# Weight loads on SyncE's queue and threshold rows on GpSimd's in a fused attention and feed-forward kernel

## The chip, the cores and the metric

The kernel runs on one core of a Trainium2 chip. The metric is device time in microseconds (us) of one execution, the median of several. Engines are named as in the profile: PE (TensorE matmul), PEld (its weight loads), DVE (VectorE), ACT (ScalarE), POOL (GpSimd), SP (SyncE, which here only issues DMAs). A DMA is issued by an engine's instruction; the transfer itself runs on 16 DMA engines that all queues share.

## The reference, cut to what matters

```python
# q, k, v: (8, 8, 576, 64) float32; tau = 0.02
scale = 1.0 / np.sqrt(q.shape[-1])
scores = scale * np.matmul(q, k.transpose(0, 1, 3, 2))
thresh = np.max(scores, axis=-1, keepdims=True) - tau
scores = np.where(scores >= thresh, scores, -1000000000.0)
scores = scores - np.max(scores, axis=-1, keepdims=True)
attn = np.exp(scores)
attn = attn / (np.sum(attn, axis=-1, keepdims=True) + 1e-09)
attn_out = np.matmul(attn, v)
# (B, H, S, D) -> x: (4608, 512)
h = x @ w_in                                  # w_in:  (512, 2048)
g = h * (1.0 / (1.0 + np.exp(-1.702 * h)))
out = g @ w_out                               # w_out: (2048, 512)
```

`w_in` and `w_out` reach the kernel as 64-bit floats and are made 32-bit on the chip.

## The kernel before

**Attention** goes by pairs of heads: 8 batches of 4 pairs, 32 pairs n = 0 to 31. For each pair SP loads q and k (`load_qk`, four DMAs of 72 KB each, in pieces of 128 bytes; only k of pair 0 is issued by ACT) and v (`load_v`, four of 144 KB). DVE transposes q and k (`prep`, L502). PE makes the transposed scores in nine tiles of 64 keys (`scores`, L518), ACT copies them out of PSUM (`keep`, L535), DVE takes maxima over keys (`in_groups`, L541; `over_tiles`, `over_halves`). The row of thresholds must then stand in every partition: `turn_rows` (L585) transposes it, `row_out` (L631, two DMAs) writes it to DRAM, `row_in` (L640, two DMAs of 144 KB) reads it back into all partitions, tile `mb`. Pair 2 does this on DVE alone (`spread_max`). DVE subtracts it (`sub`, L646, five instructions per pair), ACT masks and exponentiates (`mask` L652, `exps` L656). PE multiplies with v (`values`, L667, tile `pv`). Sums over keys come from PE for pairs 0 to 4 (`sums_by_pe`, tile `den`; DVE then `one_row`, `spread_sums`), later from DVE, and then their reciprocals go out and in through DRAM too (`sums_out` L734, `sums_in` L741). `place_x` (L769) writes the normalised result as a part of x, tile `xT`.

**Weights** come in 32 pieces of 128 x 512 values, 512 KB each, 16 of `w_in` first. `load_w` (L451) issues one from GpSimd into a staging place: eight halves of stages in the tile `w_out` and four places (`w64`) in `arena`. Six steps make a piece 32-bit: `cv_ex` (L459), `cv_frac` (L477), `cv_join` (L484) and `cv_end` (L491) on DVE, `cv_power` and `cv_power2` (L466, L470) on ACT. A place is free for the next piece after `cv_end`. The first six loads wait for `hold`, a one-column copy on GpSimd that reads k of pair 3 after its transpose.

**Feed-forward** goes by blocks of 256 tokens. The first two blocks (`first_blocks`) need pairs 0 to 3 placed and the weights: 128 matmuls of `mm1_0` (L824), 16 activations (`tanh` on ACT, `gelu_0` on DVE, L830), 64 matmuls of `mm2` (L806). After them ACT and GpSimd form sums of `w_out` (`t_minus` L931; `t_plus` L935, a DMA that adds, issued by GpSimd). The following blocks (`feed_forward`, L784 and L796; `second`, L975, with DVE reads at L997) use a scheme with seven products in place of eight and GpSimd sums (L941 to L954); the last four blocks use it in both layers. Block b begins when the pairs of its batch are placed.

**Order.** Nothing of this order is written out by hand. Each step is a `task` with an engine, an assumed cost, a rank, the tasks that it follows, and buffers that it takes and gives back. `run_in_order` plays the whole kernel with these costs, and on each engine issues the ready task of the lowest rank. So the instruction order on every engine is fixed when the program is built, and on the chip each engine runs its list in order, waiting by semaphores. The rank of an attention task is the pair's number plus a bias by step (tables `EARLY`, `SECOND`, `LATER` for pairs 0 to 3, 4 to 7, and later ones), that of a weight task comes from `W_RANK` plus a bias of table `CV`. Transfers are played on two assumed movers, "DMS" for SP's queue and "DMW" for GpSimd's, which share by `SHARE` when both are busy.

From pair 4 on q and k of pair n are loaded after the row of pair n - 2 has been issued (`behind`). From pair 7 on the scores of pair n are interleaved with the values of pair n - 2 (`JOINT`).

Of the kernel before, what the change touches and what calls it, by code (L numbers as in the profile page):

```python
# [30 lines left out]
def kernel(  # L31
# [83 lines left out]
    gap = const.tile([P, 1], FP32, name="gap")  # L115
    stop = const.tile([P, 1], FP32, name="stop")
    minus = const.tile([P, 2, KT], FP32, name="minus")
# [11 lines left out]
    for x in ("raw0", "raw1", "qkT0", "qkT1", "mb"):  # L129
# [5 lines left out]
    EARLY = {  # L135
        "exps": -4.07,
        "in_groups": 22.01,
        "keep": -79.06,
        "load_qk": 12.29,
        "load_v": 22.73,  # L140
        "mask": -2.64,
        "one_row": 11.94,
        "over_halves": -68.94,
        "over_tiles": -10.94,
        "place_x": -9.91,
        "prep": 31.46,
        "row_in": 266.46,
        "row_out": -20.89,
        "scores_run": -78.01,
        "spread_max": 21.18,  # L150
        "spread_sums": -40.19,
        "sub": 20.98,
        "sums_by_pe": 115.71,
        "turn_rows": 8.92,
        "values": 5.45,
        "w_sum": -2.55,
    }
    SECOND = {
        "exps": -5.9,
        "in_groups": 272.61,  # L160
        "keep": 24.39,
        "load_qk": 24.22,
        "load_v": 275.36,
        "mask": 21.81,
        "one_row": 3.96,
        "over_halves": 26.26,
        "over_tiles": -69.17,
        "place_x": 24.28,
        "prep": 26.2,
        "row_in": 3.22,  # L170
        "row_out": 27.26,
        "scores_run": 11.9,
        "spread_sums": -33.61,
        "sub": 26.97,
        "sums_by_pe": -17.24,
        "sums_in": -40.32,
        "sums_out": -33.4,
        "turn_rows": 86.46,
        "turn_sums": 113.15,
        "values": -68.38,  # L180
    }
    LATER = {
        "exps": -16.87,
        "in_groups": 287.56,
        "keep": -81.02,
        "load_qk": -69.87,
        "load_v": -9.77,
        "mask": 15.33,
        "over_halves": 8.05,
        "over_tiles": -2.37,  # L190
        "place_x": -12.35,
        "prep": -40.12,
        "row_in": 27.6,
        "row_out": -2.41,
        "scores_run": 27.98,
        "sub": 29.43,
        "sums_in": -21.09,
        "sums_out": -40.82,
        "turn_rows": -18.77,
        "turn_sums": -16.08,  # L200
        "values": -68.99,
        "x_sum": -2.89,
    }
    CV = {
        "cv_end": 29.51,
        "cv_ex": 20.82,
        "cv_frac": 114.8,
        "cv_join": -10.06,
        "cv_power": 12.8,
        "cv_power2": 5.12,  # L210
        "load_w": -4.52,
    }
# [18 lines left out]

    SHARE = (0.22, 0.6)

# [205 lines left out]
    def load_w(i):  # L439
        dst, src, c, j = pieces[i]  # L440
        dram = src[ts(c, P), ts(j, WC)]
        if not wide:
            nc.gpsimd.dma_start(out=dst[:, c, ts(j, WC)], in_=dram)
            return
        at = staged(i)
        if at in W64:
            t = arena[:, ts(W64.index(at), 2 * WC)]
        else:
            t = w_out[:, ts(HALVES.index(at), 2), :].rearrange("p a b -> p (a b)")
        t = t.bitcast(U32)  # L450
        nc.gpsimd.dma_start(out=t, in_=dram.bitcast(U32), max_dma_last_dim=1024)  # L451
        t = t.rearrange("p (c w) -> p c w", w=2)
        cv[i] = t[:, :, 1], t[:, :, 0], dst[:, c, ts(j, WC)]
# [41 lines left out]

    held_k = {}
    mats, sT, stats, mbs, rows, pss = {}, {}, {}, {}, {}, {}

    def prep(n, which):

        dst = home(n, f"qkT{which}")
        nc.vector.transpose(out=dst, in_=raws.pop((n, which)))  # L502
        mats[n, which] = dst
        if which:
            held_k[n] = dst

    def hold(n):

        nc.gpsimd.tensor_copy(out=stop, in_=held_k[n][:, 0:1])

# [115 lines left out]


    def row_out(n):
        rows[n] = dram.tile([2, S], FP32, name="row", tag="row", bufs=2)
        for c in range(2):  # L630
            nc.sync.dma_start(  # L631
                out=rows[n][c : c + 1].rearrange("o (g i) -> (o g) i", i=32),
                in_=flat[1][ds(c * KT, QB)],
            )

    def row_in(n):
        mb = home(n, "mb")
        row = rows.pop(n)
        for c in range(2):
            nc.sync.dma_start(out=mb[ts(c, KT)], in_=row[c : c + 1].to_broadcast([KT, S]))  # L640
        mbs[n] = mb
# [89 lines left out]
    def sums_out(n):  # L731
        rcs[n] = dram.tile([2, 2, SH], FP32, name="row_s", tag="row_s", bufs=2)
        for c in range(2):
            nc.sync.dma_start(  # L734
                out=rcs[n][c].rearrange("h (g i) -> (h g) i", i=32), in_=flat_s[1][ds(c * KT, QB)]
            )

    def sums_in(n):
        rc, row = seat("rc"), rcs.pop(n)
        for h in range(2):  # L740
            nc.sync.dma_start(  # L741
                out=rc[ts(h, D)].rearrange("p (c s) -> p c s", c=2),
# [309 lines left out]
    SUMS_BY_DMA = range(5, NP)  # L1052
    LEAD = 6
    WHOLE = 6

# [3 lines left out]

    W_RANK = (21.04, 13.12, 21.54, 8.44, 155.39, -7.77)  # L1060
    W_TIME = 1.9
    ready_w, w_loads = [], []
    for i in range(len(pieces)):
# [7 lines left out]
        place = (staged(i),)  # L1071
        a = task("POOL", 0.6, rank, load_w, i, after=w_loads[-1:], take=place)
        w_loads.append(a)
        a = transfer("DMW", W_TIME, a)

# [177 lines left out]
    lvs = []  # L1253
    exped, loaded, summed = {}, {}, {}

# [21 lines left out]
    for n in range(NP):  # L1277
# [145 lines left out]
        if n not in SUMS_BY_PE:  # L1423
# [5 lines left out]
            if n in SUMS_BY_DMA:  # L1429
                a = task("DVE", 1.46, r, turn_sums, n, after=[a], take=("row_s",))  # L1430
                a = transfer("DMS", 0.3, task("SP", 0.65, r, sums_out, n, after=[a]))
                a = task("SP", 1.2, r, sums_in, n, after=[a], take=("rc",))
                summed[n] = transfer("DMS", 0.7, a, 1, give=("row_s",))
            else:
# [42 lines left out]
```

## Time and profile before

| What | us |
|---|---|
| Runs shown: median (lowest to highest, 3 runs) | 1313.77 (1311.2 to 1315.54) |
| Profiled execution, its own time | 1316.25 |
| Profiled execution, span from first to last instruction | 1314.4 |
| PE busy in the span | 1261.8 |
| DVE busy | 1007.4 |
| ACT busy | 667.0 |
| POOL busy | 242.7 |
| Granted PE clock, mean over the span | 0.988 |

DMA traffic by queue, in packets, MB and share of the time of 16 DMA engines:

```profile
q1 hardware_dynamic: 180476, 64.30, 20.8%
q0 software_dynamic: 8800, 20.97, 6.1%
```

q1 is the queue of DMAs that SP issues, q0 that of GpSimd's; a third one (q10) carries ACT's one load. Issuing a DMA is not counted as busy time. A matmul that is listed as 128x256 f32 counts twice in the trace, since it runs in two passes. Line numbers in the profile are those of the kernel before.

### The profile page before, as it was taken

The numbers are of one execution on the slowest core, as the hardware profiler recorded it, in microseconds if no ns is written. First come the engines' busy times: TensorE is split into PE (matmuls) and PEld (weight loads), VectorE is DVE, ScalarE is ACT, GpSimd is POOL, SyncE is SP. The second block draws the span as 40 slices with busy tenths as digits, with TensorE's granted clock in tenths as the row PEclk, the third lists the DMA queues.
The fourth block names the chain that finished last, engine by engine and source line by source line (L and its number), as shares of the span: only waits on it lengthen the run. The fifth ranks groups of instructions, "written<-read, shape, count | busy, mean of one in ns | idle before, by whom it ended". The sixth has DMA issues, their size and how long they took to land.

```text
span 1314.4 us, 22775 instructions
## 1 busy us (share of the span) xinstructions
PE 1261.8 (96%) x9128; PEld 980.3 (75%) x9128; DVE 1007.4 (77%) x1601; ACT 667.0 (51%) x862; POOL 242.7 (18%) x269
## 2 busy tenths in 40 slices
PE   5777999999999999999999999999999999999998
PEld 2635764466787777777778887777777778888887
DVE  7899898999987888788787877777887864652642
ACT  4897666876745545555554554454655540210210
POOL 1102010012030211213021302021121217120120
PEclk8888999999999999999999999999999999999999
DMA  6724356453322222112222222222122110000000
GB/s 125 230 65 151 79 175 109 98 119 73 89 64 71 55 55 71 46 54 55 57 43 71 55 71 56 71 50 63 44 61 54 31 51 9 9 1 30 3 0 32
DMA packets 191749, 87.01 MB, mean 66 GB/s; under 512 B 159772, under 2 KB 170780, under 8 KB 191644
## 3 DMA queue, kind: packets, MB, share of 16 engines
q1 hardware_dynamic: 180476, 64.30, 20.8%
q0 software_dynamic: 8800, 20.97, 6.1%
q8 instruction: 71, 1.16, 0.4%
q10 hardware_dynamic: 2368, 0.30, 0.2%
q14 instruction: 34, 0.28, 0.1%
HBM read 71.63 MB, written 9.70 MB: 62 GB/s over the span
## 4 chain that ended last, share of the span: by engine, by line
PE 72%; DVE 15%; DMA 6%; ACT 3%; issue 2%; SPq 2%; DVEq 0%; ACTq 0%
PE ops L975 25%; PE hps L784 21%; PE pv L667 8%; PE ps L518 7%; PE ps L889 4%; DVE part L541 4%; PE ps L975 4%; DVE arena L646 3%; PE ops L889 3%; DMA row<-flat 2%; DMA arena<-row 2%; ACT arena L656 1%; DVE arena L502 1%; DMA arena<-in_k_dram 1%; SPq L398 1%
## 5 line engine op out<-in xcount | busy, mean ns | idle before, releaser
L541 DVE TRANSPOSE_TENSOR_REDUCE part<-arena 128x36 f32<-128x1152 f32 (+1 forms) x295 | 357.6, 1237 | 41.7 <-ACT arena L535 32.3
L784 PE MATMUL hps<-xT,w_in 128*128 128x256 f32 x1536 | 337.2, 380 | 1.3 <-DVE arena L796 1.2
L784 PEld LDWEIGHTS hps<-xT,w_in 128*128 128x128 f32 x1536 | 290.6, 190 | 46.9 <-issue 5.7
L652 ACT ACTIVATE arena<-arena 128x1152 f32<-128x1152 f32 (+1 forms) x160 | 169.6, 1060 | 133.1 <-DVE arena L646 132.8
L535 ACT COPY arena<-ps 128x576 f32<-128x576 f32 x288 | 170.8, 647 | 120.8 <-PE ps L518 120.8
L646 DVE TENSOR_TENSOR arena<-arena 128x1152 f32<-128x1152 f32 (+1 forms) x158 | 200.8, 1316 | 21.1 <-DMA arena<-row 20.9
L975 PE MATMUL ops<-w_out,arena 128*128 128x256 f32 x896 | 204.6, 383 | 3.0 <-DVE osb L997 1.9
L656 ACT ACTIVATE arena<-arena,shift,scl 128x1152 f32<-128x1152 f32 (+1 forms) x160 | 200.6, 1254 | 4.0
L518 PE MATMUL ps<-arena 64*64 64x288 f32 x2304 | 175.0, 420 | 23.9 <-DVE arena L502 10.9
L975 PEld LDWEIGHTS ops<-w_out,arena 128*128 128x128 f32 x896 | 170.2, 191 | 31.5 <-DVE arena L796 3.1
L941 POOL TENSOR_TENSOR arena<-arena 128x256 f32<-128x256 f32 x56 | 49.0, 874 | 646.8 <-DVE arena L796 545.1
L667 PE MATMUL pv<-arena 64*64 64x288 f32 x2176 | 159.9, 407 | 0.0
L793 ACT ACTIVATE th<-hps 128x512 f32<-128x512 f32 x112 | 66.2, 591 | 175.2 <-PE hps L784 157.7
L518 PEld LDWEIGHTS ps<-arena 64*64 64x64 f32 x2304 | 87.4, 138 | 86.8 <-ACT arena L535 21.2
L975 PE MATMUL ops<-arena 128*128 128x256 f32 x672 | 150.6, 380 | 0.0
L975 PEld LDWEIGHTS ops<-arena 128*128 128x128 f32 x672 | 127.3, 190 | 19.3 <-issue 2.2
L667 PEld LDWEIGHTS pv<-arena 64*64 64x64 f32 x2176 | 81.6, 133 | 53.9 <-issue 9.6
L997 DVE SCALAR_TENSOR_TENSOR osb<-ops,osb 128x256 f32<-128x256 f32 x98 | 39.4, 414 | 98.4 <-PE ops L975 92.3
L796 DVE SCALAR_TENSOR_TENSOR arena<-th,hps 128x512 f32<-128x512 f32 x96 | 64.4, 670 | 39.4 <-ACT th L793 39.3
L824 PE MATMUL hps<-xT,w_in 128*128 128x256 f32 x256 | 59.1, 390 | 7.4 <-DVE w_in L491 3.7
L824 PEld LDWEIGHTS hps<-xT,w_in 128*128 128x128 f32 x256 | 49.2, 195 | 17.5 <-DVE arena L830 4.9
L909 ACT ACTIVATE th<-arena 128x512 f32<-128x512 f32 x32 | 20.3, 636 | 72.5 <-DVE arena L905 72.5
(118 smaller groups left out, 1085.2 us busy)
## 6 DMA issues: line engine op xcount, KB each, us to landing
arena<-in_v_dram SPq DMA_DIRECT2D x128, 144.0 KB
arena<-in_q_dram SPq DMA_DIRECT2D x128, 72.0 KB
out_dram<-osb SPq DMA_DIRECT2D x36, 256.0 KB
arena<-in_k_dram SPq DMA_DIRECT2D x124, 72.0 KB
arena<-row SPq DMA_DIRECT2D x62, 144.0 KB
arena<-row_s SPq DMA_DIRECT2D x54, 144.0 KB
w_out<-in_moe_w_in_dram POOLq DMA_DIRECT2D x12, 512.0 KB, 7.4
arena<-in_moe_w_out_dram POOLq DMA_DIRECT2D x12, 512.0 KB, 7.5
```

Source lines behind the costliest of these rows:

```text
L518: nc.tensor.matmul(ps[ts(c, KT), h, 0:SH], lhsT=mats[n, 1][ts(h, D), ts(j, KT)], rhs=mats[n, 0][ts(h, D), ts(c, SH)], start=True, stop=True,)
L535: nc.scalar.copy(out=sT[n, t][:, u], in_=pss.pop((n, j))[:, :, 0:SH])
L541: nc.vector.tensor_reduce(out=stats[n, op][:, t * 2 * QB : min(2 * t + 2, NK) * QB], in_=sT[n, t].rearrange("p u h (g d) -> p (u h g) d", ...
L646: engine.tensor_tensor(out=s, in0=s, in1=mbs[n].unsqueeze(1).to_broadcast(list(s.shape)), op=ALU.subtract)
L652: nc.scalar.activation(out=s, in_=s, func=AF.Prelu, alpha=STEEP)
L656: nc.scalar.activation(out=s, in_=s, func=AF.Exp, scale=scl, bias=shift)
L667: nc.tensor.matmul(o[c][ts(h, D), 0:SH], lhsT=left(j, h)[ts(c, KT)], rhs=sT[n, t][ts(c, KT), u, h, :], start=(j == 0), stop=(j == NK - 1),)
L784: nc.tensor.matmul(hidden[j][:, ts(f, BLK)], lhsT=w_in[:, c, ds((f * HF + j) * P, P)], rhs=xTs[blk][:, c, :], start=(c == 0), stop=(c == N ...
L793: nc.scalar.activation(out=ths[j], in_=hidden[j], func=AF.Tanh, scale=GELU_SCALE / 2)
L824: nc.tensor.matmul(hidden[j][:, ts(i, BLK)], lhsT=w_in[:, c, ts(j, P)], rhs=xTs[i][:, c, :], start=(c == 0), stop=(c == NDC - 1),)
L889: nc.tensor.matmul(places[j, x], lhsT=left[:, c, ts(j, P)], rhs=right[:, c, :], start=(c == 0), stop=(c == 1),)
L975: nc.tensor.matmul(banks[blk][k][:, ts(o, HM)], lhsT=left[:, j, :], rhs=right[:, j, :], start=(j == 0), stop=(j == HF - 1),)
```

## The change

- `load_w` issues the weights from SP, in the queue of q, k and v. Its task goes to SP, its transfer to mover "DMS" (kind 2); `SHARE` gets a third entry.
- `hold`, the tile `stop` and the waits for them are gone: the first weights may be loaded from the start.
- `row_queue(n)`: for pairs 0 to 7 `row_out`, `row_in`, `sums_out` and `sums_in` are issued by GpSimd, for later pairs by SP as before.
- `behind`: q and k of pair n wait for the transposes of an earlier pair instead of the row of pair n - 2, where that row is issued by GpSimd or n is 2.
- All biases in `EARLY`, `SECOND`, `LATER` and `CV`, the six numbers of `W_RANK`, and `W_TIME` are other numbers, so the whole order is played anew.

```diff
-    SHARE = (0.22, 0.6)
+    SHARE = (0.15, 0.5, 0.6)
...
-        nc.gpsimd.dma_start(out=t, in_=dram.bitcast(U32), max_dma_last_dim=1024)
+        nc.sync.dma_start(out=t, in_=dram.bitcast(U32))
...
-        if which:
-            held_k[n] = dst
-
-    def hold(n):
-
-        nc.gpsimd.tensor_copy(out=stop, in_=held_k[n][:, 0:1])
...
+    def row_queue(n):
+        return nc.gpsimd if n in ROWS_BY_POOL else nc.sync
+
     def row_out(n):
         rows[n] = dram.tile([2, S], FP32, name="row", tag="row", bufs=2)
         for c in range(2):
-            nc.sync.dma_start(
+            row_queue(n).dma_start(
...
-            nc.sync.dma_start(out=mb[ts(c, KT)], in_=row[c : c + 1].to_broadcast([KT, S]))
+            row_queue(n).dma_start(out=mb[ts(c, KT)], in_=row[c : c + 1].to_broadcast([KT, S]))
...
+    ROWS_BY_POOL = range(8)
     WHOLE = 6
...
-    W_RANK = (21.04, 13.12, 21.54, 8.44, 155.39, -7.77)
-    W_TIME = 1.9
+    W_RANK = (-17.54, -19.75, 3.69, 13.93, 26.33, -28.4)
+    W_TIME = 1.6
...
-        a = task("POOL", 0.6, rank, load_w, i, after=w_loads[-1:], take=place)
+        a = task("SP", 0.65, rank, load_w, i, after=w_loads[-1:], take=place)
         w_loads.append(a)
-        a = transfer("DMW", W_TIME, a)
+        a = transfer("DMS", W_TIME, a, 2)
...
+        rq = ("POOL", 1.4, "DMW", 2.2) if n in ROWS_BY_POOL else ("SP", 1.0, "DMS", 1.7)
...
-        behind = [spread[n - 2]] if n >= NPAIR else []
+        behind = [spread[n - 2]] if n >= NPAIR and n - 2 not in ROWS_BY_POOL else preps[n - 1 if n > 3 else n - 2] if n in (2, *range(4, NP)) else []
...
+        preps.append([pq, pk])
         if n == 0:
             tasks[tau_done][5].extend([pq, pk])
-        if n == 3:
-
-
-            h = task("POOL", 0.3, FIRST, hold, n, after=[pk])
-            for a in w_loads[0:6]:
-                tasks[a][5].append(h)
...
-            a = transfer("DMS", 0.3, task("SP", 0.65, r, row_out, n, after=[a]))
-            spread[n] = task("SP", 1.1, r, row_in, n, after=[a], take=own(n, "mb"))
-            m = transfer("DMS", 0.7, spread[n], 1, give=("row",))
+            a = transfer(rq[2], 0.3, task(rq[0], 0.65 * rq[1], r, row_out, n, after=[a]))
+            spread[n] = task(rq[0], 1.1 * rq[1], r, row_in, n, after=[a], take=own(n, "mb"))
+            m = transfer(rq[2], 0.7, spread[n], 1, give=("row",), lag=rq[3])
```

Left out: the tables of biases (all values replaced) and `sums_out`, `sums_in` with their tasks, changed in the same way as `row_out` and `row_in`. Lists of the built programs show what this does to the order. SP's list now begins with four weight pieces, then q of pair 0, q and k of pair 1, six pieces, q and k of pairs 2 and 3, six pieces, and only then v of pairs 0 and 1. DVE's list begins with the conversion of the first four pieces, then the transposes of pair 0. On PE the 128 matmuls of `mm1_0`, broken up by attention of pairs 4 and 6 before, stand in one run.

More of the change, by code (lines that the diff above doesn't have):

```diff
@@ L115 @@
     gap = const.tile([P, 1], FP32, name="gap")
-    stop = const.tile([P, 1], FP32, name="stop")
     minus = const.tile([P, 2, KT], FP32, name="minus")
@@ L135 @@
     EARLY = {
[L136 to L153, printed above, removed]
@@ L154 @@
-        "turn_rows": 8.92,
-        "values": 5.45,
-        "w_sum": -2.55,
+        "exps": 47.12,
+        "in_groups": 31.3,
+        "keep": 32.74,
+        "load_qk": 29.52,
+        "load_v": 88.91,
+        "mask": 47.59,
+        "one_row": -13.82,
+        "over_halves": 23.69,
+        "over_tiles": -19.38,
+        "place_x": 36.77,
+        "prep": -75.13,
+        "row_in": -12.15,
+        "row_out": 37.49,
+        "scores_run": 5.02,
+        "spread_max": -15.22,
+        "spread_sums": 32.66,
@@ L157 @@
+        "sub": -13.77,
+        "sums_by_pe": 11.61,
+        "turn_rows": -17.79,
+        "values": 9.46,
+        "w_sum": 36.74,
     }
     SECOND = {
[L159 to L180, printed above, removed]
+        "exps": 48.41,
+        "in_groups": 90.77,
+        "keep": -52.88,
+        "load_qk": 12.53,
+        "load_v": 67.07,
+        "mask": 27.44,
+        "one_row": 59.42,
+        "over_halves": 22.95,
+        "over_tiles": 6.12,
+        "place_x": 27.27,
@@ L181 @@
+        "prep": 41.33,
+        "row_in": 35.7,
+        "row_out": 20.9,
+        "scores_run": 30.56,
+        "spread_sums": -25.02,
+        "sub": 67.34,
+        "sums_by_pe": -4.59,
+        "sums_in": 9.14,
+        "sums_out": 58.99,
+        "turn_rows": 12.71,
+        "turn_sums": 66.39,
+        "values": 56.01,
     }
     LATER = {
[L183 to L202, printed above, removed]
+        "exps": 20.37,
+        "in_groups": 85.93,
+        "keep": 12.29,
+        "load_qk": 56.34,
+        "load_v": 4.91,
@@ L203 @@
+        "mask": 45.29,
+        "over_halves": 13.04,
+        "over_tiles": 11.11,
+        "place_x": 43.96,
+        "prep": 29.75,
+        "row_in": -12.01,
+        "row_out": 12.27,
+        "scores_run": 19.69,
+        "sub": 73.39,
+        "sums_in": 27.57,
+        "sums_out": 40.94,
+        "turn_rows": 21.08,
+        "turn_sums": 42.06,
+        "values": -14.78,
+        "x_sum": 62.94,
     }
     CV = {
-        "cv_end": 29.51,
-        "cv_ex": 20.82,
-        "cv_frac": 114.8,
@@ L208 @@
[L208 to L211, printed above, removed]
+        "cv_end": 47.56,
+        "cv_ex": 38.81,
+        "cv_frac": 65.22,
+        "cv_join": 80.5,
+        "cv_power": 48.25,
+        "cv_power2": -13.93,
+        "load_w": 28.32,
     }
@@ L493, in cv_end @@
         )
-    held_k = {}
     mats, sT, stats, mbs, rows, pss = {}, {}, {}, {}, {}, {}
@@ L733, in sums_out @@
         for c in range(2):
-            nc.sync.dma_start(
+            row_queue(n).dma_start(
                 out=rcs[n][c].rearrange("h (g i) -> (h g) i", i=32), in_=flat_s[1][ds(c * KT, QB)]
@@ L740, in sums_in @@
         for h in range(2):
-            nc.sync.dma_start(
+            row_queue(n).dma_start(
                 out=rc[ts(h, D)].rearrange("p (c s) -> p c s", c=2),
@@ L1253 @@
     lvs = []
-    exped, loaded, summed = {}, {}, {}
+    exped, loaded, summed, preps = {}, {}, {}, []
     def valued(n, pv):
@@ L1430 @@
                 a = task("DVE", 1.46, r, turn_sums, n, after=[a], take=("row_s",))
-                a = transfer("DMS", 0.3, task("SP", 0.65, r, sums_out, n, after=[a]))
-                a = task("SP", 1.2, r, sums_in, n, after=[a], take=("rc",))
-                summed[n] = transfer("DMS", 0.7, a, 1, give=("row_s",))
+                a = transfer(rq[2], 0.3, task(rq[0], 0.65 * rq[1], r, sums_out, n, after=[a]))
+                a = task(rq[0], 1.2 * rq[1], r, sums_in, n, after=[a], take=("rc",))
+                summed[n] = transfer(rq[2], 0.7, a, 1, give=("row_s",), lag=rq[3])
             else:
```

## The prediction, made before the changed kernel had run

> **What bounds the kernel now.** I read the page first, its busy times and its 40 slices (32.9 us each).
>
> ```profile
> PE 1261.8 (96%) x9128; PEld 980.3 (75%) x9128; DVE 1007.4 (77%) x1601; ACT 667.0 (51%) x862; POOL 242.7 (18%) x269
> ...
> PE   5777999999999999999999999999999999999998
> ...
> DVE  7899898999987888788787877777887864652642
> ```
>
> PE is full from the fifth slice on; before that DVE is. Busy times of whole stretches fix the border:
>
> ```profile
> 0.00:30.39 30.39, 14.49 (x164) 6.83 (x168) 20.97 (x37) 12.62 (x22) 3.52 (x22) 0.90 0.70 127
> 30.39:116.43 86.04, 62.83 (x849) 39.06 (x841) 77.97 (x133) 79.49 (x99) 8.41 (x12) 0.90 0.45 123
> 116.43:340.00 223.57, 214.87 (x1504) 142.50 (x1505) 209.11 (x335) 149.94 (x194) 35.61 (x38) 0.99 0.53 122
> 340.00:1314.40 974.40, 969.65 (x6618) 791.94 (x6616) 699.34 (x1100) 424.99 (x549) 195.18 (x198) 1.00 0.19 47
> ```
>
> (Columns: stretch, length, busy PE, PEld, DVE, ACT, POOL, granted clock, DMA share, GB/s.) Of PE's 52.6 us without work, 39.1 lie before 116.43, 8.7 before 340, 4.7 in the 974 us after. So only the first 340 us can give or lose much. The timeline of PE says what 116.43 is and what it waited for:
>
> ```profile
> 116.43 22.67 PE L824 MATMUL hps<-xT,w_in 128*128 128x256 f32 x96 [3.73 <-DVE w_in L491]
> 140.94 10.98 PE L824 MATMUL hps<-xT,w_in 128*128 128x256 f32 x48 [1.84 <-DVE arena L830]
> ...
> 296.04 7.17 PE L784 MATMUL hps<-xT,w_in 128*128 128x256 f32 x32 [1.25 <-DVE arena L796]
> ...
> 337.49 5.41 PE L975 MATMUL ops<-w_out,arena 128*128 128x256 f32 x16 [1.89 <-DVE osb L997]
> ```
>
> The first feed-forward matmul starts at 116.43, held by DVE (a weight's last conversion step, L491). DVE is late for its own reasons; its waits up to 345 us:
>
> ```profile
> DVE arena L646 <- DMA arena<-row: 13.8, 5, 5.7
> DVE arena L502 <- DMA arena<-in_q_dram: 7.3, 1, 7.3
> ```
>
> 7.3 us pass before the first q lands; the subtractions (L646) wait five times for threshold rows, 5.7 us for pair 1 at 38.7 to 44.5. In the chain that wait is row out and row in, under the first twelve weights:
>
> ```profile
> 30.81 4.55 DMA row<-flat
> 35.38 8.99 DMA arena<-row
> 44.46 5.83 DVE arena L646 x5
> ```
>
> **What the change leaves alone.** The instruction lists of the two kernels hold the same matmuls with the same 64 switches between attention and feed-forward; before the first feed-forward matmul stand the same scores, sums and values, and from some 285 us of PE work on PE's order is identical. DVE too has the same work in front of it: summing the means of the page's fifth part over DVE's list, 109.7 us in both (placement of pair 3 now; before, the last step of weight piece 0). DVE runs such sums faster than their means: work 48.2 to 109.7 took 59.23 to 116.29, 57.1 us for 61.5, factor 0.93. So the new time is the old, plus the shift of that first matmul, plus the shift of PE's waits behind it.
>
> **Part 1: weights first, in SP's queue.** Four pieces stand ahead of q of pair 0, six more ahead of pair 2, six ahead of v. Removed: POOL's copy (hold, 0.18 us at 29.3) and the wait of weights for pair 3; POOL loses 32 issues of 0.75 us, SP gets them (0.65 by its q rows, 2.13 to 3.37 us for four), 21 us on an engine that otherwise waits.
>
> ```profile
> L451 POOL DMA_DIRECT2D w_out<-in_moe_w_in_dram x12: 751/751/782, 29.8 to 118.9; - x12
> ...
> DMA to landing us min/median/max: 3.8/8.4/14.4
> ```
>
> A lone piece takes 3.8 us from issue, and at the 346 GB/s that the windows give for 120 to 132 us each piece behind it 1.5 us more: landings near 4.6, 6.1, 7.6, 9.1. DVE converts them (0.42 + 0.43 + 0.70 + 0.68 each) in the time in which it waited. q of pair 0 flows behind them: 0.295 MB at 150 GB/s (the window at 4 to 16 us) is 2.0 us; its last DMA waits besides for an earlier one (each of SP's loads waits for the load eight before it, by the list), and k of pair 0, on ACT, now stands behind the first conversion's activation. I take 13.5 us for q landed, first scores at 15 (8.8 before).
> The same arithmetic for the rest: k of pair 1 at 19, six weights flow to 28, q and k of pairs 2 and 3 (2.0 us each plus latency, k of 3 issued by 35.6) land by 37.8. DVE's list puts the transposes of pair 3 ahead of the first subtraction, which so starts near 39.5 (30.39 before): 9.1 later, with 30.3 us of work done against 22.9, worth 7.4 x 0.93 = 6.9. Debt +2.2 us. Bounds: -1.3 (loads land 3.5 us sooner, DVE then held by its own work) to +10 (weights at the 227 GB/s that v reaches at 68 to 70 us, 2.3 us a piece: ten pieces, 0.8 us longer each).
>
> **Part 2: rows by GpSimd.** Pairs 0, 1, 3 to 7 send rows out and in (28 DMAs), pairs 5 to 7 also sums (12): 40 x 0.75 = 30 us on POOL, busy 18%. On SP the trip took 6.0 us from 242.5 (row end to landing) with little else moving and 14.0 for pair 1. On POOL the trace shows none. Lower bound 6; upper 14; between: 2 issues 1.5, landing 3.4 behind the issue (tau's load by GpSimd, 4.1 from its issue), 2 issues 1.5, landing 3.0 (the lone weight's 3.8 less its issue): 9.4. I take 9.4, for it is nearest to calm rows of the same engine. DVE's work between row and subtraction is 9.6, 9.2 and 8.8 us by means, 8.9, 8.6 and 8.2 in time, for pairs 0, 1, 3. Pair 0 hides (its subtraction waits for loads); pairs 1 and 3 wait 0.8 and 1.2. With 1.0 for sums that ACT delivers late (from its first mask near 41 to pair 3's last exponential ACT has 68 us of activations and ends at 109, with 3.5 of sums and placement behind it on DVE), waits come to 3.0 where 5.7 were: -2.7.
> What else sits on POOL: sums in of pair 5 stand behind the first T transfer (L935), which waits for two activations of 1.05 us; placement of pair 5 is 10 us of work later. Nothing, unless that cover goes; then some 2 us on DVE.
> GpSimd's issues meet DVE's work: 32 weight issues took 751 to 912 ns while DVE was 90% busy. The Trainium skill ("SBUF — State Buffer", on DVE blocking DMAs) says the opposite could happen: GpSimd writes descriptors through a port that some DVE instructions lock, 620 ns becoming about 3100. The trace disagrees so far. At 3.1 us for each of a trip's four issues the trip would be 9.4 us longer, by estimate from that page, and the time beyond (b) below, whose chance holds it.
>
> First matmul: 116.4 + 2.2 - 2.7 = **115.9**.
>
> **Part 3: new ranks, behind that.** PE now runs its 128 first-layer products in a row (3.45 us for each activation), with 57.9 x 0.93 = 53.9 us of DVE between first and last of 16 activations against 51.8 of PE: +2.1. Values of pair 5 stand 80.5 us of PE behind the start (89.1 before); with 2.1 for switches and 2.1 of waits PE is there at +84.7, and DVE, which must have summed pair 5 (95.6 us by means, x 0.93), at +88.9: 4.2 more. Beyond, q, k and rows come sooner than before; I take 0.6. Waits 6.9, against 1.84, 1.74, 1.48, 0.34, 1.25, 1.89 (8.5): -1.6. Bounds: 0 and 15 (the three later pairs each wait like pair 5).
>
> **Sum.** -0.5 - 1.6 = -2.1 on the profiled execution's own 1316.25 (span 1314.4 and 1.85 around it): 1314.2. The runs' median lies 2.5 below that execution, so **1311.7**. About 0.3%, 3.9 us, is what a measurement here can tell from no change.
>
> **Rivals.**
> (a) The waits vanish: loads at their early bound and rows hidden, -1.3 - 5.7 = -7.0 for the start, and PE's waits behind it 5.5, -3.0: -10, **1304**. For: DVE idles 14.5 us between 116 and 340, 8.1 of them for rows. Against: DVE and PE run level there, so one holds the other.
> (b) Slower by rows: the trip over GpSimd takes the 14.0 us of pair 1 before, for its packets share the engines with weights as before. Pairs 0, 1, 3 wait 5.1, 5.4, 5.8, 17.3 with the sums in place of 3.0: **1326**; a trip of 12 gives 1320. It decides from 10.3 us, where the sum above is used up; each further us costs three. For: the same two streams met at 31 to 44 us. Against: weights now come in bursts with gaps.
> (c) Slower by the single queue: weights at 235 GB/s, debt +10 for +2.2: **1319.5**, more with a wait for v of pair 0, which stands behind sixteen pieces. It decides from 0.2 us longer a piece. For: in order behind each other, and the eighth-load wait. Against: 4096-byte packets took 188 ns on 16 engines, 349 GB/s.
> (d) The change does not do what it says: "not held back" is taken over by the eighth-load wait, and what is gained at the start DVE takes back in the run of activations: no change, **1313.8**.
>
> **Chances.** Forecast 0.38 (own range 1306 to 1317; of it a third below 1309.8), (a) 0.22, (b) 0.14, (c) 0.14, (d) 0.12. Faster by over 0.3%: 0.12 + 0.22 + 0.03 = 0.37; within: 0.26 + 0.08 = 0.34; slower: 0.28 + 0.01 = 0.29. The range reaches to both sides' cases: 1301 to 1323.
>
> **What would show it.** First scores near 15 us; first subtraction 38 to 41; first feed-forward matmul 113 to 119; DVE's waits for rows up to 345 us under 6 in all; PE's waits from there to 340 near 6. Wrong if that matmul starts before 110 or after 122, if GpSimd's issues take much over 0.75 us, or if PE loses more than 8 us after 340.

## The result: slower by 0.8%

| | median us (lowest to highest, runs) | profiled execution, its span |
|---|---|---|
| before | 1312.08 (1311.2 to 1315.54, 5) | 1316.25, 1314.4 |
| changed | 1322.82 (1320.91 to 1326.52, 5) | 1326.52, 1324.7 |

The ratio is 1.0078, with a 95% interval from 1.0056 to 1.0100: a loss of 10.7 us where a gain of 2.1 was forecast. Both profiled executions lie some 4 us above their medians, so the two traces can be compared with each other.

The page of the changed kernel, busy times and slices of 33.1 us:

```profile
PE 1263.5 (95%) x9128; PEld 973.7 (74%) x9128; DVE 1006.5 (76%) x1601; ACT 665.1 (50%) x862; POOL 236.8 (18%) x276
...
PE   3688999899999999999999999999999999999998
...
DVE  7798997888987888877787877777887873652642
```

The work is the same. PE's first three slices are 3, 6, 8 in tenths. Stretches cut at the same events as in the prediction (first subtraction, first feed-forward matmul, 340 us, end):

```profile
0.00:41.55 41.55, 17.84 (x208) 8.47 (x208) 28.38 (x48) 21.74 (x36) 4.92 (x24) 0.92 0.88 209
41.55:122.25 80.70, 61.03 (x800) 32.67 (x800) 71.74 (x128) 71.37 (x87) 4.33 (x8) 0.87 0.46 117
122.25:340.00 217.75, 206.90 (x1472) 135.07 (x1469) 195.79 (x311) 143.85 (x190) 30.23 (x44) 0.98 0.44 102
340.00:1324.70 984.70, 977.75 (x6654) 797.51 (x6652) 710.63 (x1118) 428.18 (x551) 197.27 (x200) 1.00 0.19 47
```

The third number after the length is DVE's busy time. Up to the first subtraction DVE is not busy for 41.55 - 28.38 = 13.2 us (9.4 before); from there to the first feed-forward matmul for 9.0 (8.1 before). Its work up to that matmul is 100.1 us (98.9 before). So 3.75 + 0.9 + 1.2 = 5.8: the matmul starts at 122.25 instead of 116.43. The timeline of PE from there on (start, length, and in brackets the wait ahead of it with what ended it):

```profile
122.25 55.61 PE L819 MATMUL hps<-xT,w_in 128*128 128x256 f32 x256
196.39 1.98 PE L801 MATMUL ops<-w_out,arena 128*128 128x512 f32 x4 [2.39 <-DVE w_out L490]
258.04 2.20 PE L510 MATMUL ps<-arena 64*64 64x288 f32 x16 [6.02 <-ACT arena L527]
313.31 0.72 PE L510 MATMUL ps<-arena 64*64 64x288 f32 x8 [0.57 <-ACT arena L527]
322.30 3.72 PE L779 MATMUL hps<-xT,w_in 128*128 128x256 f32 x16 [1.17 <-DVE arena L791]
326.68 3.29 PE L970 MATMUL ops<-w_out,arena 128*128 128x256 f32 x14 [0.66 <-DVE arena L791]
351.01 7.17 PE L970 MATMUL ops<-arena 128*128 128x256 f32 x32 [1.14 <-DVE osb L992]
370.88 1.25 PE L510 MATMUL ps<-arena 64*64 64x288 f32 x16 [0.99 <-ACT arena L527]
```

These waits sum to 12.9 us where 8.5 were. 5.8 + 4.4 = 10.2 of the 10.3 us between the two spans: two places hold nearly the whole loss, the start and the stretch to some 370 us. (The feed-forward matmuls that start at 367.28 before start at 376.93 now, 9.65 us later.)

DVE's waits up to 122.25 (total, times, longest):

```profile
DVE w_in L458 <- DMA w_out<-in_moe_w_in_dram: 4.8, 1, 4.8
DVE arena L641 <- DMA arena<-row: 3.7, 2, 3.4
DVE arena L500 <- DMA arena<-in_q_dram: 3.2, 2, 2.0
DVE r L693 <- PE den L662: 3.0, 2, 2.5
DVE arena L500 <- DMA arena<-in_k_dram: 2.5, 3, 1.2
DVE w_in L490 <- ACT w_in L469: 1.7, 1, 1.7
```

Before, one wait of 7.3 for q, one of 1.0 for k and one of 5.7 for a row stood here. Now there are eleven smaller ones, and those for loads and weights come to 12.2 us (4.8 + 3.2 + 2.5 + 1.7).

How far one execution can be trusted here is shown by a run below, a_sums_sync, whose program is the same as the changed kernel's up to that matmul. Its timeline has

```profile
120.00 55.52 PE L819 MATMUL hps<-xT,w_in 128*128 128x256 f32 x256
```

which is 2.25 us sooner, with the first subtraction at 40.97. So differences of some 2 us in this start, between two traces, say nothing, and the loss of the start is 3.6 to 5.8 us.

### The profile page after: what moved, and what is told of

It is laid out like the page before. It is cut to its first block, busy times and chain, and to the rows that moved or that the text cites. A ratio compares the mean times of both kernels' runs of the same rounds, so it can differ in the third digit from the quotient of the medians.

```text
span 1324.7 us, 22760 instructions
## 1 busy us (share of the span) xinstructions
PE 1263.5 (95%) x9128; PEld 973.7 (74%) x9128; DVE 1006.5 (76%) x1601; ACT 665.1 (50%) x862; POOL 236.8 (18%) x276
## 4 chain that ended last, share of the span: by engine, by line
PE 72%; DVE 13%; ACT 7%; DMA 5%; issue 2%; SPq 1%; POOL 0%; DVEq 0%; POOLq 0%
PE ops L970 23%; PE hps L779 20%; PE pv L662 8%; PE ps L510 8%; PE ps L884 4%; DVE part L533 4%; PE ps L970 4%; DVE arena L641 4%; PE ops L884 3%; ACT arena L651 3%; ACT arena L647 2%; ACT arena L527 1%; DMA arena<-row 1%; DMA arena<-row_s 1%; DMA arena<-in_k_dram 1%
## 5 line engine op out<-in xcount | busy, mean ns | idle before, releaser
L779 PE MATMUL hps<-xT,w_in 128*128 128x256 f32 x1536 | 337.0, 380 | 1.2 <-DVE arena L791 1.2
L779 PEld LDWEIGHTS hps<-xT,w_in 128*128 128x128 f32 x1536 | 290.8, 190 | 46.3 <-issue 5.3
L801 PE MATMUL ops<-w_out,arena 128*128 128x512 f32 x128 | 57.1, 599 | 2.4 <-DVE w_out L490 2.4
L949 POOL TENSOR_TENSOR arena<-arena 128x512 f32<-128x512 f32 x28 | 37.6, 1347 | 109.8 <-PE ops L970 109.8
L904 ACT ACTIVATE th<-arena 128x512 f32<-128x512 f32 x32 | 20.3, 634 | 72.6 <-DVE arena L900 72.6
```

The costliest lines, as they stand in the source:

```text
L779: nc.tensor.matmul(hidden[j][:, ts(f, BLK)], lhsT=w_in[:, c, ds((f * HF + j) * P, P)], rhs=xTs[blk][:, c, :], start=(c == 0), stop=(c == N ...
```

## The experiments

All are compared with the kernel before, which was run beside each of them on the same chip. Its medians there went from 1313.1 to 1314.1, so between runs on different chips the ratios are the better comparison. "Order" means the instruction lists that `run_in_order` writes; changing only the engine that issues a DMA leaves them as they are, though not what each load waits for. For the last seven the played list is edited by hand: the steps are collected, a few are moved, and then they are issued.

| Run | Order | Weights | Rows | Median us | Ratio (95%) |
|---|---|---|---|---|---|
| a_order_only | changed | GpSimd | SP | 1342.4 | 1.0211 (1.0193 to 1.0229) |
| a_weights_gpsimd | changed | GpSimd | GpSimd | 1342.4 | 1.0216 (1.0199 to 1.0232) |
| a_rows_sync | changed | SP | SP | 1330.3 | 1.0121 (1.0101 to 1.0141) |
| a_sums_sync | changed | SP | GpSimd, sums SP | 1320.2 | 1.0042 (1.0028 to 1.0056) |
| b_weights_sync | before | SP | SP | 1314.5 | 1.0006 (0.9997 to 1.0015) |
| b_queues | before | SP | GpSimd | 1323.7 | 1.0077 (1.0064 to 1.0091) |
| b_rows_gpsimd | before | GpSimd | GpSimd | 1332.6 | 1.0149 (1.0136 to 1.0162) |
| a_q0_first | changed, q and k of pair 0 first | SP | GpSimd | 1324.2 | 1.0078 (1.0065 to 1.0091) |
| a_weights_behind_qk | changed, 4 to 9 behind k of pair 3 | SP | GpSimd | 1322.9 | 1.0070 (1.0056 to 1.0085) |
| a_weights_behind_sums | the same | SP | GpSimd, sums SP | 1320.8 | 1.0053 (1.0038 to 1.0069) |
| a_row0_ahead | changed, 4 to 15 behind row of pair 0 | SP | pair 0 and sums SP | 1321.0 | 1.0056 (1.0041 to 1.0071) |
| b_rows_ahead | before, weights behind row of pair 1 | SP | SP | 1310.6 | 0.9980 (0.9970 to 0.9990) |
| b_hold_row | before, weights behind row of pair 1 | GpSimd | SP | 1311.5 | 0.9987 (0.9974 to 1.0001) |
| b_piece_order | as b_rows_ahead, pieces 0 to 3 first | SP | SP | 1307.7 | 0.9956 (0.9941 to 0.9971) |

### Each queue by itself, in the changed order

```diff
-        return nc.gpsimd if n in ROWS_BY_POOL else nc.sync     # a_rows_sync, a_order_only
+        return nc.sync
...
-        nc.sync.dma_start(out=t, in_=dram.bitcast(U32))        # a_weights_gpsimd, a_order_only
+        nc.gpsimd.dma_start(out=t, in_=dram.bitcast(U32), max_dma_last_dim=1024)
...
-            row_queue(n).dma_start(                            # a_sums_sync: sums_out and sums_in
+            nc.sync.dma_start(
```

> The changed kernel with both queue changes undone and its new ranks kept: weights issued by GpSimd, threshold rows and sums by SyncE, every instruction in the order of the changed kernel; there is no hold. If the new order by itself is the loss (ACT copying pair 4 ahead of the masks of pair 3, DVE taking weights ahead of the q of pair 0), this stays near 1322 us with the first feed-forward matmul at 120 to 123. If the queues are the loss (single queue at the start +4, T transfers ahead of sums +6), it comes to 1311 to 1314 with the first feed-forward matmul near 117 and no wait of TensorE over 4 us behind it. A third way: the weights, with no hold and on their old queue, slow the q and k of the first pairs as they did before a hold was there, and it is slower than the changed kernel.

> The changed kernel with the rows and the rows of sums back on SyncE, in the same order; weights stay on SyncE's queue. If the queue shared with the two T transfers costs the 6.16 us wait of the values of pair 5 and through it TensorE's 6.02 us at 258, that wait falls to under 2 and the time by 4 to 6 us, to 1317-1319. If rows behind the queue of weights and v (SyncE waits for a load eight back before it issues) come later than over GpSimd, VectorE's waits for threshold rows before 345 us grow over the 6.2 us of the changed kernel, the first feed-forward matmul moves past 122 and the gain is eaten: 1322 or more.

> The changed kernel with only the rows of sums (pairs 5 to 7) back on SyncE; threshold rows stay on GpSimd. If sums that queue behind a T transfer are the cause of TensorE's wait of 6.02 us at 258, the time falls by 4 to 6 us, to 1317-1319, with the first feed-forward matmul at 122 as in the changed kernel. If TensorE's wait there comes from the new order (ACT's exponentials late), VectorE's wait goes and TensorE's stays: 1322.

> The changed kernel with the weights back on GpSimd's queue, not held back, same order; rows and sums stay on GpSimd. If the single queue with q, k and v costs the start (first subtraction at 41.55, first feed-forward matmul at 122), q and k come earlier with the weights on a queue of their own: first subtraction at 36 to 39, first matmul at 118 to 120, 3 us off. If the queue isn't what holds them but the transfers' rate and VectorE's order (weights ahead of q), the first subtraction stays at 41 or later. Rows behind weights on GpSimd's queue may wait longer: then VectorE's waits for rows rise over 6.2 us and the time over 1323.

a_sums_sync went the way that the queue theory expected: 2.6 us by the two medians, 0.36% or 4.7 us by the two ratios. A second pair of runs that differs in the sums alone, on one chip (a_weights_behind_qk and a_weights_behind_sums, below), gives 2.1. So the gain is 2 to 5 us, where 4 to 6 were expected. In the other three the ways named last came true: undoing the queue of the weights or of the rows in this order makes it worse. With both undone (a_order_only) it is as slow as with the weights alone, 1342.4. So the loss isn't the sum of a loss by order and a loss by queues: in the new order, which has no hold, the new queues gain some 20 us, and in the old order (below) they lose 10.

With the weights on GpSimd the start falls apart. ACT's timeline in a_weights_gpsimd:

```profile
10.23 0.72 ACT L465 ACTIVATE w_in<-w_in,rebias 128x512 f32<-128x512 int32 x1 [7.99 <-DVE w_in L458]
10.23 9.39 ACTq L397 DMA_DIRECT2D arena<-in_k_dram  x4
19.73 0.72 ACT L469 ACTIVATE w_in<-w_in,rebias 128x512 int32<-128x512 f32 x1 [8.78 <-issue]
```

The first weight lands at 9.8 us instead of 4.8 (GpSimd issues it at 3.62, SP at 0.75). The four loads of k of pair 0 then take 9.39 us to issue (2.81 in the changed kernel), while the DMA engines move 304 to 340 GB/s, weights for the most part. The list of the built program says why: a load of SP or ACT waits for the load eight before it among these two engines' loads. With the weights gone from SP these eight are q of pairs 0 and 1, so each of the four loads of k waits for a load of q to land; in the changed kernel three of the four wait for none. ACT's next activation stands behind them, DVE waits for it for 7.5 us, and the first feed-forward matmul comes at 135.0. In a_order_only it is the same (9.52 us of issue, 7.75 of waiting), then DVE waits 9.8 us for q, and the matmul comes at 137.40. That the single queue is the loss (theory one of a_weights_gpsimd) is refuted for this order.

With the rows on SP they stand behind other bytes. SP's and DVE's timelines in a_rows_sync:

```profile
36.78 0.87 SPq L626 DMA_DIRECT2D row<-flat  x2
37.70 0.97 SPq L450 DMA_DIRECT2D arena<-in_moe_w_in_dram  x2
38.71 1.52 SPq L450 DMA_DIRECT2D w_out<-in_moe_w_in_dram  x3
40.32 1.83 SPq L635 DMA_DIRECT2D arena<-row  x2
```

```profile
51.64 5.16 DVE L641 TENSOR_TENSOR arena<-arena 128x1152 f32<-128x1152 f32 x4 [10.76 <-DMA arena<-row]
```

The row of pair 0 goes in at 40.32 behind five pieces of 512 KB just issued, and lands 11.3 us later.

The sums. GpSimd's timeline in the changed kernel (durations are issue times), and the wait on DVE:

```profile
211.55 1.01 POOL L729 DMA_DIRECT2D row_s<-flat_s  x2 [44.51 <-DVE flat_s L724]
212.72 1.66 POOL L930 DMA_DIRECT2D arena<-w_out  x1 [0.16 <-issue]
214.97 1.25 POOL L736 DMA_DIRECT2D arena<-row_s  x2 [0.59 <-DMA row_s<-flat_s]
219.01 1.06 POOL L626 DMA_DIRECT2D row<-flat  x2 [2.79 <-DVE flat L577]
226.35 1.06 POOL L635 DMA_DIRECT2D arena<-row  x2 [6.28 <-DMA row<-flat]
```

```profile
225.65 0.95 DVE L764 TENSOR_TENSOR xT<-pv,arena 128x192 f32<-128x192 f32 x4 [6.16 <-DMA arena<-row_s]
```

The T transfer (L930, 1 MB, which adds as it goes; 8.9 to 10.9 us from issue to landing) is issued between sums out and sums in of pair 5. Sums in, issued at 214.97, land at 225.6, and the next row out, issued by 220.07, lands 6.28 us later at 226.35. With sums on SP DVE waits 3.3 us at this place, and PE 3.15 in place of 6.02; PE then waits 3.48 at 307 where it waited 0.57:

```profile
220.40 0.95 DVE L764 TENSOR_TENSOR xT<-pv,arena 128x192 f32<-128x192 f32 x4 [3.28 <-DMA arena<-row_s]
252.79 1.25 PE L510 MATMUL ps<-arena 64*64 64x288 f32 x16 [3.15 <-ACT arena L527]
306.94 2.20 PE L510 MATMUL ps<-arena 64*64 64x288 f32 x16 [3.48 <-ACT arena L527]
```

PE's waits behind the first feed-forward matmul come to 10.3 instead of 12.9. The other runs of the changed order with the weights on SP agree: 10.4 to 11.0 with sums on SP (a_weights_behind_sums, a_row0_ahead, a_rows_sync), 11.9 and 13.1 with sums on GpSimd (a_weights_behind_qk, a_q0_first).

### The queues in the order of before

```diff
-        nc.gpsimd.dma_start(out=t, in_=dram.bitcast(U32), max_dma_last_dim=1024)   # weights
+        nc.sync.dma_start(out=t, in_=dram.bitcast(U32))
...
-        nc.gpsimd.tensor_copy(out=stop, in_=held_k[n][:, 0:1])
+        pass
...
-            nc.sync.dma_start(                      # rows: row_out, row_in, sums_out, sums_in
+            row_queue(n).dma_start(                 # GpSimd for n < 8
```

> The kernel before, its ranks and its order kept, with the queues of the changed kernel: weights issued by SyncE (so behind the q and k that stand ahead of them in SyncE's stream, with no hold on GpSimd), threshold rows and sums of the first eight pairs by GpSimd. If the queues are the loss of the changed kernel (rows 8 to 12 us per trip over GpSimd, sums behind the T transfers, one queue for all loads), the time goes up by 4 to 10 us, to 1316-1322. If the new order is the loss, it stays within 3 us of 1312. The first feed-forward matmul stands at 116 before and at 122 in the changed kernel.

> The kernel before with only the rows and sums of the first eight pairs on GpSimd, where the weights also are, in the order of before. If a row waits behind the weights that stand ahead of it in GpSimd's stream (each some 2 us of transfer), VectorE's waits for rows before 345 us grow over the 13.8 us of the kernel before, and the time goes to 1318 or more. If GpSimd takes rows between the weights at no loss, rows wait less than over SyncE, and the time is 1308-1312.

> The kernel before with only the weights moved to SyncE, in its own order, with no hold; rows and sums stay on SyncE behind them. In the order of the changed kernel this pair of queues gave a wait of 10.8 us for the first row. If that comes from rows standing behind loads on SyncE, it is seen here too, where weights stand between rows: VectorE's waits for rows over 13.8 us and 1316-1325. If weights by SyncE come sooner than over GpSimd at no cost to the rows, the first feed-forward matmul loses its wait of 3.73 us for the weights: 1308-1311.

In this order moving the weights alone costs nothing that can be told, and moving the rows as well costs another 9 us: the queues without the new order lose as much as the changed kernel. Rows on GpSimd behind the weights there (b_rows_gpsimd) cost 19. In b_queues the first feed-forward matmul stands at 116.56, as before; the loss comes behind it (PE's waits to 370 us are 13.8 against 8.5), and DVE waits there for rows 3.0 us at 195 and, behind the second T transfer on GpSimd's queue, 6.0 at 236, where b_weights_sync has one wait of 2.7.

```profile
235.92 2.63 DVE L649 TENSOR_TENSOR arena<-arena 128x1152 f32<-128x1152 f32 x2 [5.98 <-DMA arena<-row]
```

The wait at 195 has no T transfer ahead of it, and why that row is late isn't shown. (The profiled execution of b_queues is its fastest, so its trace differs by 5 us from that of before and the medians by 10.)

The row of pair 1 tells more. DVE's line of its first subtractions in b_weights_sync, b_queues and b_rows_gpsimd, in this order:

```profile
46.80 5.17 DVE L646 TENSOR_TENSOR arena<-arena 128x1152 f32<-128x1152 f32 x4 [7.99 <-DMA arena<-row]
```

```profile
43.69 5.17 DVE L649 TENSOR_TENSOR arena<-arena 128x1152 f32<-128x1152 f32 x4 [5.56 <-DMA arena<-row]
```

```profile
48.66 5.16 DVE L649 TENSOR_TENSOR arena<-arena 128x1152 f32<-128x1152 f32 x4 [10.07 <-DMA arena<-row]
```

In one queue with the weights the row waits 8.0 (SP) or 10.1 us (GpSimd); in another queue than the weights 5.6, and 5.7 in the kernel before, whose rows went by SP and weights by GpSimd. So another queue helps, but less than half. The Trainium skill ("DMA: Bandwidth & Descriptors", on queues, rings and completion order) has each DMA engine take packets from its queues in turn, so a transfer in a queue of its own shares and doesn't stand behind; these four waits agree with that.

### The place of the bytes

```diff
+        held_w = [x for x in played if x[0] is load_w and x[1][0] < 10]     # b_rows_ahead
+        played[:] = [x for x in played if x not in held_w]
+        at = next(i for i, x in enumerate(played) if x[0] is row_in and x[1][0] == 1)
+        played[at + 1 : at + 1] = held_w
...
-        nc.gpsimd.tensor_copy(out=stop, in_=held_k[n][:, 0:1])              # b_hold_row: hold moved likewise
+        nc.gpsimd.tensor_copy(out=stop, in_=mbs[1][:, 0:1])
```

> The kernel before, in its own order, weights on SyncE and no hold, as in the run in which only the weights were moved (1314.5), but with the first ten weights behind the threshold row of pair 1 in SyncE's stream instead of around it. If a row is late because weights' bytes stand ahead of it on the rings (8.0 us of VectorE's wait at 46.8 there, 5.7 at 44.5 in the kernel before), that wait falls under 2 us, and the first feed-forward matmul, which VectorE's work sets, comes 4 to 6 us sooner than the 116.4 of the kernel before: 1306-1310. If the row is late for its own trip, the wait stays over 4 and the time at 1312-1315. If the weights, now issued from some 37 us, come late, VectorE waits for them near 77 us and the time is 1315 or more.

> The kernel before with nothing but its hold moved: GpSimd's copy that releases the first ten weights reads the threshold row of pair 1 instead of the k of pair 3; weights stay on GpSimd, rows on SyncE. If what counts is that the weights' bytes come behind the row, and not which queue carries them, VectorE's wait of 5.7 us for that row falls under 2 us and the time is that of the run with rows ahead in one queue, 1309-1312. If the one queue for all loads has a gain of its own (weights in packets that take less time, no issue work on GpSimd), it is 1313 or more.

SP's and DVE's timelines in b_rows_ahead (its line numbers are 7 higher than those of before):

```profile
30.49 0.63 SPq L638 DMA_DIRECT2D row<-flat  x2
31.69 2.02 SPq L647 DMA_DIRECT2D arena<-row  x2
33.77 2.08 SPq L458 DMA_DIRECT2D w_out<-in_moe_w_in_dram  x4
35.89 1.17 SPq L458 DMA_DIRECT2D arena<-in_moe_w_in_dram  x2
```

```profile
38.64 5.13 DVE L653 TENSOR_TENSOR arena<-arena 128x1152 f32<-128x1152 f32 x4
```

The row is out and in ahead of the first weight, and the subtraction at 38.64 has no wait. The first feed-forward matmul comes at 112.65; with the weights on GpSimd (b_hold_row) at 111.92, and there too the subtraction, at 38.05, has no wait. The two runs' medians differ by 0.9 us and their intervals overlap. So it is the place of the weights' bytes, behind the row, that is worth some 2 us, and which queue carries them can't be told apart. Only b_rows_ahead is clear of noise: the interval of b_hold_row ends at 1.0001. The medians moved less than the traces, whose executions are the fastest of their runs.

### The same in the changed order

```diff
+        ahead = [x for x in played if x[0] in (load_qk, prep) and x[1][0] == 0]         # a_q0_first
+        played[:] = ahead + [x for x in played if x not in ahead]
...
+        held_w = [x for x in played if x[0] is load_w and 4 <= x[1][0] < 10]            # a_weights_behind_*
+        played[:] = [x for x in played if x not in held_w]
+        at = next(i for i, x in enumerate(played) if x[0] is load_qk and x[1][:2] == (3, 1))
+        played[at + 1 : at + 1] = held_w
...
+        held_w = [x for x in played if x[0] is load_w and 4 <= x[1][0] < 16]            # a_row0_ahead
+        at = next(i for i, x in enumerate(played) if x[0] is row_in and x[1][0] == 0)
...
-        return nc.gpsimd if n in ROWS_BY_POOL else nc.sync                              # a_row0_ahead
+        return nc.gpsimd if n in ROWS_BY_POOL and n else nc.sync
```

> The changed kernel with the loads of q and k of pair 0 issued ahead of the first weights and their two transposes ahead of the weights on VectorE; all else in the same order. If weights ahead of q are what the start costs, the first scores come at 9 instead of 16.4, VectorE's 4.8 us wait for the first weight is spent on nothing longer than the wait for q, and the first feed-forward matmul comes 3 to 6 us sooner, at 116-119: 1317-1320. If VectorE's work up to the first feed-forward matmul is what counts (some 100 us of it, whatever comes first) and the wait for q is as long as that for the first weight, only the first scores move, and the first feed-forward matmul stays at 120-122: 1321-1323.

> The changed kernel with weights 4 to 9 put on SyncE behind the k of pair 3 instead of ahead of the q of pair 2 (SyncE's stream alone is changed; the first four weights still lead). If those six weights hold q and k of pairs 2 and 3 (issued from 20.8 to 37.2 us, VectorE waiting 1.2 + 0.6 + 2.0 + 0.8 us for them and ACT 7.1 for their scores), the waits go, the first subtraction comes at 37 to 38 instead of 41.55 and the first feed-forward matmul 3 to 5 us sooner, at 117-119: 1318-1320. If another wait takes their place (weights late for VectorE at 53, v late, the row of pair 1), it stays at 1321-1324.

> The same with the sums of pairs 5 to 7 on SyncE as well. If the start and the sums are two losses in places of their own, the gains add up: the 2.6 us that sums on SyncE gave alone, and what the weights behind k give alone: 1315-1318. If both feed one wait of TensorE, the sum is less than the larger of them plus 1 us.

> The changed kernel with sums on SyncE, and the threshold row of pair 0 on SyncE too, with weights 4 to 15 behind it and behind q and k of pairs 2 and 3; the other rows stay on GpSimd. With the weights behind k alone, the row of pair 0 over GpSimd met their bytes and VectorE waited 5.7 us for it (1320.8). If the place of the bytes is the cause, that wait falls under 1 us, the first subtraction comes at 36 to 38 and the time falls 3 to 6 us, to 1315-1318. If VectorE then waits as long for the row of pair 1 or for weights (its next work), it stays at 1319-1322.

None gave the start back. With q first DVE waits 6.6 us for it instead of 4.8 for a weight, and all its waits for loads and weights are 12.6 instead of 12.2. With weights 4 to 9 behind k of pair 3 those waits fall to 7.6, as expected; but the twelve pieces then pass while the row of pair 0 is on its way. DVE's first subtractions in a_weights_behind_qk:

```profile
43.54 5.83 DVE L648 TENSOR_TENSOR arena<-arena 128x1152 f32<-128x1152 f32 x5 [6.38 <-DMA arena<-row]
59.05 1.36 DVE L648 TENSOR_TENSOR arena<-arena 128x1152 f32<-128x1152 f32 x1 [0.34 <-DMA arena<-row]
```

and in a_row0_ahead, where the row of pair 0 goes ahead of them, with PE's next long wait:

```profile
36.26 5.83 DVE L648 TENSOR_TENSOR arena<-arena 128x1152 f32<-128x1152 f32 x5
56.66 1.36 DVE L648 TENSOR_TENSOR arena<-arena 128x1152 f32<-128x1152 f32 x1 [5.24 <-DMA arena<-row]
```

```profile
53.38 4.67 PE L669 MATMUL pv<-arena 64*64 64x288 f32 x30 [6.35 <-DMA arena<-in_v_dram]
```

The first subtraction comes 5.3 us sooner than in the changed kernel, and then the row of pair 1 and v of pair 0 are late in its place. In a_weights_behind_sums the two gains did not add up: its ratio, 1.0053, isn't under the 1.0042 that sums on SP gave alone. My reading, not shown by itself, is that the bytes of sixteen weights and of q, k and v of the first pairs have to pass early in this order, and each move only chooses who waits.

### What sets the first feed-forward matmul

Times in us, of each run's profiled execution; DVE's smaller waits and gaps are left out.

| Run | First feed-forward matmul | DVE busy until then | not busy | waits for loads and weights | for rows | for sums from PE |
|---|---|---|---|---|---|---|
| before | 116.43 | 98.9 | 17.5 | 8.3 | 5.7 | 0 |
| b_queues | 116.56 | 99.0 | 17.6 | 8.8 | 5.9 | 0 |
| b_weights_sync | 118.88 | 99.1 | 19.8 | 7.8 | 8.0 | 0 |
| b_rows_gpsimd | 121.33 | 99.2 | 22.1 | 8.3 | 10.1 | 0.3 |
| b_rows_ahead | 112.65 | 98.7 | 13.9 | 9.2 | 0 | 1.9 |
| changed | 122.25 | 100.1 | 22.1 | 12.2 | 3.7 | 3.0 |
| a_sums_sync | 120.00 | 99.7 | 20.3 | 11.6 | 3.1 | 2.1 |
| a_weights_behind_qk | 117.95 | 99.4 | 18.5 | 7.6 | 7.2 | 0 |
| a_row0_ahead | 120.70 | 99.2 | 21.5 | 7.9 | 5.9 | 5.3 |
| a_rows_sync | 128.85 | 99.8 | 29.0 | 10.0 | 13.9 | 0 |

DVE has 99 to 100 us of work up to that matmul in every one of them, and the matmul comes when DVE has been idle as well. If so, only an order that puts other work there can undercut it. That was the last experiment: in the kernel before, `W_RANK` falls with the piece's number, and the first twelve are converted in the order 11, 10, 3, 9, 2, 8, 7, 1, 6, 5, 0, 4. The first matmuls read pieces 0 to 3, and piece 0 is the last but one.

```diff
+        done = [x[1][0] for x in played if x[0] is cv_end and x[1][0] < 12]
+        place = dict(zip(done, sorted(done)))
+        played[:] = [(f, (place[a[0]],)) if f in steps and a[0] in place else (f, a) for f, a in played]
```

> As the run with rows ahead (1310.6), with the first twelve weights converted in the order in which the first feed-forward matmul uses them: the same instructions in the same places of VectorE and ACT, with the pieces' numbers exchanged, so that pieces 0 to 3 come first. There the first matmul waits 5.1 us for a weight converted last. If VectorE's list of work up to the first feed-forward matmul sets its start, and this order lets it start before the list is done, it comes 4 to 6 us sooner, at 107-109, and the time falls to 1304-1308. If TensorE then waits as long further on (VectorE and ACT late with gelus and scores), the gain is given back: 1309-1311.

PE's timeline of b_rows_ahead has the first line, that of b_piece_order the other two:

```profile
112.65 17.67 PE L831 MATMUL hps<-xT,w_in 128*128 128x256 f32 x69 [5.12 <-DVE w_in L498]
```

```profile
108.15 7.17 PE L835 MATMUL hps<-xT,w_in 128*128 128x256 f32 x32
118.10 12.10 PE L835 MATMUL hps<-xT,w_in 128*128 128x256 f32 x47 [2.78 <-DVE arena L841]
```

The wait of 5.12 is gone, the matmul starts at 108.15 with 95.2 us of DVE's work done, and 2.78 us are given back at the next wait for an activation. The median is 1307.7, 0.44% (0.29 to 0.59) under the kernel before and the fastest of all.

## Why the prediction was wrong

**What bounds the kernel.** Right. The loss lies in the first 370 us, and the shift of the first feed-forward matmul and the waits behind it add up to it. The forecast had -0.5 for the shift and -1.6 for the waits; +5.8 and +4.4 were measured in these traces (a shift of +3.6 in a_sums_sync, whose start is the same).

**What the change leaves alone.** Nearly: DVE had 1.2 us more work done at that matmul, since on PE 1.6 us of scores stand between the placement that it needs and the matmul. The sum had 0.

**Part 1, the loads.** The signs came near: first scores at 16.4 (15 forecast), first subtraction at 41.55 (39.5). The debt was 3.75 us, not 2.2: q and k of pairs 2 and 3 behind six pieces cost DVE 4.5 us of waits, as a_weights_behind_qk showed by taking them away. Rival (c)'s rate was wrong: in the stretches from 20 to 28 us the one queue moved 355 and 365 GB/s. A single queue as such costs nothing that can be told (b_weights_sync).

**Part 2, the rows.** The step that failed at the start: waits of 3.0 after the first subtraction where 5.7 were. They were 6.7 (3.7 for rows, 3.0 for sums), and DVE's idle time there rose by 0.9 us instead of falling by 2.7. The trip was sized at 9.4; pair 3's took 7.8 us and pair 1's 11.6, while v, q and k of other pairs passed. The trip was sized from calm rows of the issuing engine. The runs show that the bytes on the DMA engines at that moment, and whether they stand in the same queue, set much of it: in the order of before DVE waits 5.7 us for the row of pair 1 by SP beside weights by GpSimd, 5.6 with the two engines exchanged, 8.0 and 10.1 with both in one queue, and not at all when the weights, by SP or by GpSimd, come after a row by SP. A row by GpSimd ahead of the weights was not run. GpSimd's issues themselves were cheap, 0.50 to 0.69 us each under a busy DVE, where 0.75 was priced; no issue here shows the port lock of the Trainium skill's page "SBUF — State Buffer".

**Sums behind the T transfer.** "Nothing, unless that cover goes; then some 2 us on DVE" was the step that failed behind the first matmul. The cover was ten us of later work, priced against two activations; the transfer itself, 1 MB in the same queue, was not priced. DVE waited 6.2 us, PE 6.0 at 258. Sums back on SP give 2 to 5 us.

**Part 3, the waits behind.** 6.9 forecast, 12.9 measured, and the two large terms were not where they were put: the 128 products ran without a wait (2.1 forecast), the values of pair 5 came in time (4.2 forecast).

**The rivals.** Slower by rows (b) came near in time, 1320 for a trip of 12, but by luck: its rows were to wait 17.3 us with the sums before the first feed-forward matmul, and they waited 6.7. The trip doesn't slow alike for all pairs. The 14.1 us of pair 5's sums are as long as (b) has a trip, but behind a T transfer and not beside weights. (c) had the sign and the wrong price. Each was thought to act at one place, when the new order meets several.

What stays open: the changed order with its best queues (a_sums_sync) is still 8 to 10 us behind b_rows_ahead (by the ratios, by the medians). By the two traces, whose spans differ by 12.7, some 7 lie ahead of the first feed-forward matmul (120.0 against 112.65), 6 of them in DVE's idle time; three edits moved it and none removed it. Why the sums still cost DVE 3.3 us on SP, and which of the replaced biases hurts, is open too. No search for another order was made.

## What to carry to other kernels

Ask of a small transfer on the critical path which bytes stand ahead of it or beside it at the moment it is issued. Where both engines issued the same row beside weights in the other's queue (pair 1, 5.7 and 5.6 us) the engine made no difference, and moving 5 MB behind one row gained what changing queues did not. Where one in-order engine sets a stage's end, the end is its work plus its idle time: list the waits, and expect an edit that removes one to feed the next. Price a queue's other users by their whole transfer, not by the instruction that issues them. And look in the built program which earlier load each load waits for: moving loads to another queue changes that too.

## What the runs showed of the hardware

- With the same pieces of 512 KB behind the same row, the DMA engines moved 395, 419 and 412 GB/s in three stretches of 4 us from 40 us on with the pieces in SP's queue (b_rows_ahead), and 322, 356 and 349 GB/s with them in GpSimd's (b_hold_row), fully busy in both. GpSimd's loads also carry `max_dma_last_dim=1024`, so the queue and this setting aren't told apart.
- A row of thresholds that was issued while weights moved kept DVE waiting 5.6 to 5.7 us with the weights in another queue, 8.0 and 10.1 us in the same one, and not at all when it went by SP with the weights behind it.
- An adding DMA of 1 MB issued by GpSimd took 8.9 to 10.9 us to land in the changed kernel, and the sums and the row issued behind the first one in that queue landed 2 to 3 us after it (at 225.6 and 226.35, where ACT has waited for it until 223.8).
